# Loading 128 rows at a time and releasing each load by a product's place in its block of 256 TensorE instructions

## The chip, the cores and the metric

The kernel runs on one core of a Trainium2 chip. The metric is the device time of one execution in microseconds (us). TensorE is called PE below (its weight loads PEld), VectorE DVE, ScalarE ACT, GpSimd POOL and SyncE SP. SP computes nothing here: it issues nearly all of the transfers, one behind the other, in the order in which the program lists them.

## The reference, cut to what matters

Block-sparse attention over 4 batches, 8 heads and 768 rows of head size 64, followed by a soft mixture of 8 experts with 4 slots each. Everything is float32.

```python
# attention: blocks of 32 rows; each block sees its neighbours, the first and last block,
# and 3 sampled blocks; the first and the last block of queries see all keys
scores = (1 / sqrt(64)) * q @ k.T
scores = where(mask, scores, -1e9)
attn = softmax(scores)            # per row
x = (attn @ v)                    # -> 3072 x 512
# soft mixture of experts
logits = x @ phi                  # 3072 x 32
d = softmax(logits, axis=0)       # over the 3072 rows
slot_input = d.T @ x              # 32 x 512, 4 slots per expert
h = maximum(slot_input[e] @ w1[e], 0)      # w1: 8 x 512 x 1024
slot_out[e] = h @ w2[e]                    # w2: 8 x 1024 x 512
out = softmax(logits, axis=1) @ slot_out   # 3072 x 512
```

The two weight tensors are 16.8 MB each and are read once. Keys, queries and values are a few MB per batch.

## The kernel before, in words

**Attention.** The four batches run one after the other. A batch has two dense parts (the first and the last block of queries against all keys: products sd at line 730, avd at line 628) and eleven pairs of query blocks. For a pair, POOL and ACT copy the keys that the pair sees into a staging tile (kst, lines 455 to 465) and POOL copies the sampled values (vrs, line 481), PE makes the scores (s, line 536), DVE the maxima, ACT the exponentials, DVE the 32x32 transposes (ptt), and PE the products with the values (av, line 628). Every finished tile of 128 rows of x is transposed on PE (mxt, line 821); groups of four tiles go through the logits and the running softmax over rows (ml, lt, md, ms, lines 856 to 906).

**Loads.** Batch b+1's keys and values are loaded while batch b computes (`plan_loads`, line 415: `load_k` at line 339, `load_v` at line 350). Eleven weight tiles of 512 KB (`NPRE`, pool wpre) are loaded during attention (line 1049). In the last batch, 12 more tiles go into buffers that keys, values and dense probabilities no longer need: 3 in a key buffer (kw), 6 in the first value buffer (v), 3 in ptd (line 1059). After that come 3 tiles in the second key buffer (kw again, in halves of 512 columns) and all the rest, in whatever space the end of attention frees (`load_late`, line 1197, in the order `LORD`). There are 64 weight tiles in all. When attention is over, the experts' products (pf at line 1243, pso at line 1251) follow the arrival of the weights, and the output (po, line 1347) is stored in 26 transfers.

**Order of the work.** `Plan.run` (line 96) lays out the tasks of attention before anything is emitted. Each task has a cost, the engines that may do it, the tasks that it needs, buffers that it takes, and a key. The planner walks through time: at each step it takes, of the tasks that could start first, the one with the lowest key. The key is the task's place (the number n of its pair) plus an offset for its kind from the table `OFF`. So `OFF` decides the order on every engine. The result is an order per engine, written out by hand: SP too issues its transfers in that order.

**Pacing.** Loads with `pace=True` (keys and values of batches 1 to 3, the 11 early weight tiles and the 12 tiles of the last batch) are spread out in two ways. In the plan, the next may start no sooner than bytes / `RATE` after the one before (line 144; `RATE` counts MB per us). In the program, each waits for a PE instruction (lines 196 to 200): the last one of the latest PE task that ends by the plan 1.5 us before the load's planned start. The loads are cut into pieces of `LR` = 32 rows of the 128 (line 419 for keys and values of batch 1 and the keys of the others, line 1049 and 1059 for the weights). The values of batches 2 and 3 are cut in quarters of 32 rows by their layout (line 350), whatever `LR` is. As SP issues in order, what stands behind a waiting load waits too: the query tiles (q, line 330, 128 KB each, four buffers) stand between the paced loads.

Of the kernel before, what the change touches and what calls it, by code (L numbers as in the profile page):

```python
# [40 lines left out]

LD0, LD1 = 3, 12

LR, RATE = 32, 0.22

LC = 512

# [12 lines left out]
H1, HALF = 3, 4  # L60
CPES = [0, 0, 3, 3, 3, 2, 0, 0]
HEAD = -4096
SWITCH = 0.095
BACK = {"PE": 0.17, "DVE": -0.07, "ACT": -0.1, "POOL": -0.06, "SP": 0.0, "NONE": 0.0}
OFF = {"acc": 4.15, "av": 2.35, "av1": 4.1, "av2": -5, "avo": -4.9, "avo1": -5, "ce": 5, "cm": -2.05,
       "cn": 0.65, "dav": 3.7, "davo": -3.85, "dexp": 1.8, "do": 2.9, "dqk": 0.05, "dt": 4.55, "dtop": 0.85,
       "dtrn": -4.55, "exp": 2.7, "fix": 4.3, "ldq": 3.55, "lexp": -1.45, "lg": -0.55, "lo": -2.85, "lp": -5,
       "lt": 5, "ltop": -5, "qk": 0.85, "scl": 3.05, "smp": 3.9, "sum": -3.1, "top": -4.8, "trn": 0.2,
       "vst": 4.7, "xt": -2.8, "xto": -1}
E_ = mybir.EngineType  # L70
MAN = {E_.PE, E_.DVE, E_.Activation, E_.Pool}
LAG = {"PE": 0.28, "DVE": 0.08, "ACT": 0.06, "POOL": 0.1, "SP": 0.0, "NONE": 0.0}
# [10 lines left out]
class Plan:  # L83
# [6 lines left out]
    def add(self, f, opts, deps, key, acq=(), byte=0, pre=None, pace=False, kind=None, mode=None, ni=0):  # L90
        t = Task(f, opts if isinstance(opts, list) else [opts], deps, key + OFF.get(kind, 0.0), acq, byte, pre, pace,
                 kind, mode, ni)
        self.tasks.append(t)
        return t

    def run(self):
        tasks = self.tasks
        at = {e: 0.8 for e in LAG}
        dma = paced = 0.0
        mode = None  # L100
        left = {t: len(t.deps) for t in tasks}
        ready = {t: 0.0 for t in tasks}
        out = {t: [] for t in tasks}
        for t in tasks:
            for d in t.deps:
                out[d].append(t)
        slot = {p: [0.0] * n for p, n in self.pools.items()}
        held = {p: [set() for _ in range(n)] for p, n in self.pools.items()}
        nxt = {p: 0 for p in self.pools}
        queue = {p: sorted([t for t in tasks if any(q == p for q, _ in t.acq)], key=lambda t: t.key)  # L110
                 for p in self.pools if p not in self.free}
        gives = {t: [] for t in tasks}
        spans, open_ = [], {}
        avail = [t for t in tasks if not t.deps]
        order = []
        while avail:
            cand = []
            for t in avail:
                r, ok, k = ready[t], True, {}
                for p, _ in t.acq:  # L120
                    i = (nxt[p] + k.get(p, 0)) % self.pools[p]
                    k[p] = k.get(p, 0) + 1
                    if (p in queue and queue[p][0] is not t) or held[p][i]:
                        ok = False
                        break
                    r = max(r, slot[p][i])
                if ok:
                    if t.pace:
                        r = max(r, paced)

                    st, e, d = min(((max(r, at[e]), e, d) for e, d in t.opts), key=lambda z: (z[0], z[0] + z[2]))
                    if e == "PE" and t.mode and t.mode[0] != mode:
                        d += SWITCH
                    cand.append((st, t.key, st + d, t, e, d))
            assert cand, [(t.key, t.opts) for t in avail][:8]
            soon = min(c[:3] for c in cand)
            eng = min(cand, key=lambda c: c[:3])[4]
            st, _, en, t, e, d = min((c for c in cand if c[4] == eng and c[0] <= soon[0] + 0.05), key=lambda c: c[1:3])
            avail.remove(t)
            if e == "PE":  # L140
                mode = t.mode[-1] if t.mode else None
            t.start, t.eng, at[e] = st, e, en + BACK[e] + (0.11 if t.kind in ("qk", "dqk") else 0.0)
            if t.pace:
                paced = st + t.byte / RATE / 1e6
            if e == "NONE":
                t.fin = st
            elif e == "SP":
                dma = max(dma, st + 2.2) + t.byte / 0.39e6
                t.fin = dma + 1.8
            elif t.kind == "fix":  # L150
                t.fin = st + 0.1
            else:
                t.fin = en
            order.append(t)
            for p in {p for p, _ in t.acq}:
                if p in queue:
                    queue[p].pop(0)
            for p, users in t.acq:
                i = nxt[p]
                nxt[p] = (i + 1) % self.pools[p]  # L160
                held[p][i] = set(users)
                for u in users:
                    gives[u].append((p, i))
                spans.append([p, i, st, 1e9])
                open_[p, i] = spans[-1]
            for p, i in gives[t]:
                held[p][i].discard(t)
                slot[p][i] = max(slot[p][i], t.fin + LAG[e])
                if not held[p][i]:
                    open_[p, i][3] = slot[p][i]  # L170
            for o in out[t]:
                left[o] -= 1
                ready[o] = max(ready[o], t.fin + LAG[e])
                if not left[o]:
                    avail.append(o)
        assert len(order) == len(tasks), len(tasks) - len(order)

        todo = {e: [t for t in order if t.eng == e and t.pre] for e in at}
        pe_end = 0.0
        pe = []  # L180
        for t in order:
            q = todo[t.eng]
            while q and q[0].start <= t.start + 1.6:
                u = q.pop(0)
                u.vals = u.pre(u.eng)
            if t.eng == "PE":

                if (t.start > self.fill[0].fin and t.start - pe_end > 0.45
                        and sum(p == "s" and a < t.start and z > pe_end for p, _, a, z in spans) < SB):
                    self.fill[1](int((t.start - pe_end - 0.15) / 0.28))  # L190
                pe_end = t.fin
            i = t.f(t)
            if t.eng == "PE":
                last = next(i for i in reversed(self.tc.nc.cur_bb.bb.instructions) if i.engine == E_.PE)
                pe.append((t.fin, last.name))
            elif t.pace:

                name = [n for f, n in pe if f <= t.start - 1.5][-1]
                self.tc.add_manual_dep(i.ins, name, mybir.DependencyInfo(
                    mybir.DependencyClass.Sync, mybir.DependencyReason.DATA), reason="pace")  # L200


@with_exitstack
# [1241 lines left out]
```

## Time and profile before

| | |
|---|---|
| time, median of 3 executions | 310.28 us (310.16 to 313.34) |
| the profiled execution, its own time | 308.52 us |
| its span, first to last instruction | 306.7 us |
| mean granted TensorE clock | 0.971 |
| busy: PE, DVE, POOL, ACT | 279.4, 213.5, 179.2, 166.2 us |
| read from HBM, written | 56.19 MB, 6.29 MB |

The time of an execution holds some 1.8 us more than the span of its instructions. Times in the views are counted from the first instruction. A view of windows gives, for each stretch, the busy time of each engine with the number of its instructions in brackets, the granted clock, the mean busy share of the 16 DMA engines and what they moved. In a timeline, instructions of one kind that follow each other are merged to one row: start, length, engine, line, operation, tiles, count, and in square brackets the idle time ahead of them and what ended it ("issue": nothing that the profile shows). Of the transfers' queues, q1 carries the tensors and q8 what is marked "instruction".

### The profile page before, as it was taken

To read this page: it belongs to the slowest core of one execution; us is meant where nothing else is said; L and a number is where in the kernel's file an instruction comes from. 1 tells how busy PE (TensorE), PEld (TensorE's weight loads), DVE (VectorE), ACT (ScalarE), POOL (GpSimd) and SP (SyncE) were. 2 spreads that over 40 slices of the span, in tenths; PEclk is the share of its full clock that TensorE was granted. 3 is DMA by queue.
4 is the path that set the end of the run, shared out by engine and by line. 5 is a ranking of instruction groups with operands and counts; after the bars stand their busy time and mean duration, and the time that the engine had idled before them with its cause. 6 is when DMAs were issued, how large, how long until landed. Compare 5 with 4: busy or idle time off the path is not lost.

```text
span 306.7 us, 17586 instructions
## 1 busy us (share of the span) xinstructions
PE 279.4 (91%) x7159; PEld 194.0 (63%) x7159; DVE 213.5 (70%) x496; ACT 166.2 (54%) x515; POOL 179.2 (58%) x501
## 2 busy tenths in 40 slices
PE   7689997999999999999999999999999899999670
PEld 6249774775786767757777667877767643454260
DVE  4698877567997778998988979988876361113160
ACT  0875856552767787355787754695831421014250
POOL 2669589747947889583599967569657112000000
PEclk9799997999999999999999999999999999999975
DMA  7935667640357661034476320778888999999998
GB/s 245 401 124 165 193 190 215 145 138 5 95 167 210 163 186 38 5 90 141 141 197 175 116 74 21 203 200 228 216 241 286 322 372 366 390 408 408 393 338 286
DMA packets 34227, 63.62 MB, mean 207 GB/s; under 512 B 5602, under 2 KB 19043, under 8 KB 34147
## 3 DMA queue, kind: packets, MB, share of 16 engines
q1 hardware_dynamic: 34000, 62.37, 63.8%
q8 instruction: 56, 0.92, 1.3%
q14 instruction: 25, 0.20, 0.2%
q10 hardware_dynamic: 146, 0.13, 0.1%
HBM read 56.19 MB, written 6.29 MB: 204 GB/s over the span
## 4 chain that ended last, share of the span: by engine, by line
PE 45%; DMA 24%; issue 7%; POOL 6%; POOLq 5%; ACT 4%; DVE 3%; SPq 2%; ACTq 1%
PE av L628 19%; DMA w<-in_w_dram 11%; PE avd L628 7%; DMA v<-in_w_dram 7%; PE s L536 6%; POOLq L362 4%; DMA q<-in_qT_dram 4%; PE sd L730 3%; PE mxt L821 3%; POOL vrs L481 2%; DMA v<-in_vfull_dram 2%; PE po L1347 2%; POOL kst L457 2%; PE ms L906 2%; PE ml L856 2%
## 5 line engine op out<-in xcount | busy, mean ns | idle before, releaser
L481 POOL COPY vrs<-v 128x260 f32 x264 | 95.0, 405 | 27.9 <-PE av L628 19.4
L556 ACT ACTIVATE p<-s,nm 128x256 f32<-128x256 f32 x176 | 72.4, 483 | 12.6 <-DVE nm L551 11.2
L628 PE MATMUL av<-v,ptt 64*64 64x130 f32 (+2 forms) x1728 | 75.6, 287 | 0.3 <-issue 0.3
L628 PEld LDWEIGHTS av<-v,ptt 64*64 64x64 f32 (+2 forms) x1728 | 50.4, 133 | 24.3 <-issue 17.5
L563 DVE STREAM_TRANSPOSE ptt<-p 128x512 f32<-128x512 f32 x88 | 57.6, 689 | 6.2 <-ACT p L556 5.4
L551 DVE TENSOR_REDUCE nm<-s 128x2 f32<-128x512 f32 x88 | 54.9, 679 | 3.1 <-PE s L536 2.5
L536 PE MATMUL s<-kst,q 64*32 64x256 f32 x1408 | 51.2, 385 | 4.8 <-POOL kst L465 2.8
L457 POOL COPY kst<-ktile 128x384 f32<-128x384 f32 x88 | 43.1, 507 | 17.9 <-PE s L536 16.9
L628 PE MATMUL av<-vrs,ptt 64*32 64x130 f32 x2112 | 46.4, 275 | 1.7 <-issue 1.1
L463 ACT ACTIVATE kst<-ktile 128x128 f32 x177 | 40.9, 309 | 11.2 <-PE s L536 9.9
L536 PEld LDWEIGHTS s<-kst,q 64*32 64x32 f32 x1408 | 30.2, 107 | 16.9 <-POOL kst L465 3.4
L628 PEld LDWEIGHTS av<-vrs,ptt 64*32 64x32 f32 x2112 | 35.6, 105 | 4.1 <-issue 2.7
L374 ACT COPY xT<-mxt 128x512 f32<-128x512 f32 (+1 forms) x25 | 14.1, 564 | 30.3 <-PE mxt L821 30.2
L628 PE MATMUL avd<-v,ptd 64*64 64x130 f32 x768 | 23.2, 271 | 2.0 <-DVE x L623 1.8
L628 PEld LDWEIGHTS avd<-v,ptd 64*64 64x64 f32 x768 | 21.8, 132 | 4.0 <-issue 1.6
L465 POOL COPY kst<-ktile 128x128 f32 x87 | 21.9, 294 | 0.5 <-ACT dT L890 0.5
L498 ACT ACTIVATE q<-q 128x256 f32<-128x256 f32 x25 | 10.4, 424 | 17.5 <-DMA q<-in_qT_dram 17.5
L730 PE MATMUL sd<-ktile,q 64*32 64x384 f32 x256 | 18.4, 510 | 0.9 <-ACT p L556 0.5
L761 ACT ACTIVATE pd<-sd,nb 128x384 f32<-128x384 f32 x32 | 16.6, 578 | 2.6 <-DVE nb L756 2.3
L748 DVE TENSOR_REDUCE nm<-sd 128x1 f32<-128x384 f32 x32 | 16.2, 544 | 2.6 <-PE sd L730 2.6
L821 PEld LDWEIGHTS mxt<-ident,x 128*128 128x128 f32 x96 | 10.4, 143 | 11.6 <-issue 3.7
L821 PE MATMUL mxt<-ident,x 128*128 128x128 f32 x96 | 16.3, 292 | 1.1 <-DVE x L610 1.0
(120 smaller groups left out, 276.0 us busy)
## 6 DMA issues: line engine op xcount, KB each, us to landing
q<-in_qT_dram SPq DMA_DIRECT2D x47, 128.0 KB, 2.4
w<-in_w_dram SPq DMA_DIRECT2D x44, 128.0 KB, 3.2
w<-in_w_dram SPq DMA_DIRECT2D x11, 512.0 KB, 10.1
out_dram<-ob SPq DMA_DIRECT2D x22, 256.0 KB, 3.9
ktile<-in_kT_dram SPq DMA_DIRECT2D x48, 96.0 KB, 3.1
w<-in_w_dram SPq DMA_DIRECT2D x18, 256.0 KB, 6.1
v<-in_w_dram SPq DMA_DIRECT2D x24, 128.0 KB, 3.8
v<-in_w_dram SPq DMA_DIRECT2D x12, 256.0 KB, 5.4
```

What stands on the lines that cost most here:

```text
L457: POOL.tensor_copy(out=st[:, :, w:w + 96], in_=kv[:, :, (i - 1) * BLK:(i + 2) * BLK])
L463: ACT.activation(out=st[:, :, o:o + BLK], in_=src, func=AF.Copy, scale=1.0)
L465: POOL.tensor_copy(out=st[:, :, o:o + BLK], in_=src)
L481: POOL.tensor_copy(out=st[:, :, j:j + 1, :], in_=vf[:, :, ds(t.vals[j], 1), :])
L536: PE.matmul(u.s[r][32 * p:32 * p + 32, j, :], lhsT=u.q[s_, p, j, :], rhs=kd[j][0][s_, p, :], start=True, stop=True)
L551: DVE.tensor_reduce(out=u.nm[r], in_=u.s[r], axis=AX.X, op=ALU.max, negate=True)
L556: ACT.activation(out=u.p[r][:, j, :], in_=u.s[r][:, j, :], func=AF.Exp, bias=u.nm[r][:, j:j + 1], scale=1.0)
L563: DVE.transpose(out=T.pt[r][:, :, 2 * w:2 * w + 2, :].rearrange("p k j q -> p j k q"), in_=u.p[r].rearrange("p j (k q) -> p j k q", k=8))
L628: PE.matmul(av[:, r * 2 * D1:(r + 1) * 2 * D1].rearrange("p (a d) -> p a d", a=2), lhsT=lhsT, rhs=rhs, start=start, stop=stop)
L730: PE.matmul(u.s[r][k][32 * p:32 * p + 32, :], lhsT=T.dq.q[s_, p, j, :], rhs=kt[s_, p, 384 * k:384 * (k + 1)], start=True, stop=True)
L761: ACT.activation(out=u.p[r][k], in_=u.s[r][k], func=AF.Exp, bias=u.nb[r], scale=1.0)
L821: PE.transpose(T.px[:, c, :], T.x[:, c * P:(c + 1) * P], ident)
```

## The change

Five things are edited; the tables below are the whole of it.

1. `LR` goes from 32 to 128: a paced load moves all 128 rows at once, 512 KB for a weight tile where it was four pieces of 128 KB, 384 KB for a quarter of a batch's keys where it was four pieces of 96 KB, and so for the values of batch 1. The quarters of the values of batches 2 and 3 stay as they are. `RATE` goes from 0.22 to 0.18.
2. The planner counts PE instructions and keeps, in blocks of 256, a time `fetched`: a PE task that crosses the border of a block is lengthened if `fetched` lies later than the crossing, and each crossing sets `fetched` anew (`FETCH`, 3.5 us after the crossing, at least 3.8 us after the one before).
3. While the program is emitted, each PE instruction is entered in a list with its running number (2 for a transpose, 4 for another product, times `MORE` = 1.0092 for instructions that are not counted) and its planned time.
4. A paced load no longer waits for the end of a task 1.5 us ahead of its planned start. It waits for a product that stands `QUIET` = 50 instructions behind a border (number 191 + 256 k): the latest border that by the plan lies at least 0.3 us ahead of the load's planned start. Loads with planned starts in the same block wait for the same product.
5. All 35 offsets of `OFF` are new, so the order on all the engines is a new one.

```diff
-LR, RATE = 32, 0.22
+LR, RATE = 128, 0.18
+
+FIRST, BLOCK, MORE, QUIET = 191, 256, 1.0092, 50
...
-SWITCH = 0.095
+SWITCH, FETCH = 0.095, (3.5, 3.8)
...
-OFF = {"acc": 4.15, "av": 2.35, "av1": 4.1, "av2": -5, "avo": -4.9, "avo1": -5, "ce": 5, "cm": -2.05,
-       "cn": 0.65, "dav": 3.7, "davo": -3.85, "dexp": 1.8, "do": 2.9, "dqk": 0.05, "dt": 4.55, "dtop": 0.85,
-       "dtrn": -4.55, "exp": 2.7, "fix": 4.3, "ldq": 3.55, "lexp": -1.45, "lg": -0.55, "lo": -2.85, "lp": -5,
-       "lt": 5, "ltop": -5, "qk": 0.85, "scl": 3.05, "smp": 3.9, "sum": -3.1, "top": -4.8, "trn": 0.2,
-       "vst": 4.7, "xt": -2.8, "xto": -1}
+OFF = {"acc": 5, "av": -0.35, "av1": 0.75, "av2": -2.35, "avo": -4.7, "avo1": -3.4, "ce": -1.4, "cm": -1.65,
+       "cn": 5, "dav": 0.8, "davo": 4.5, "dexp": -5, "do": 1.75, "dqk": 0.4, "dt": -1.85, "dtop": -1.55,
+       "dtrn": -2.75, "exp": -5, "fix": -2.75, "ldq": 1.2, "lexp": -1.95, "lg": 5, "lo": 1.85, "lp": 0.05,
+       "lt": -5, "ltop": -4, "qk": -0.05, "scl": 4.55, "smp": -3.85, "sum": 4.45, "top": -2, "trn": -0.15,
+       "vst": -3.7, "xt": 4.6, "xto": 0.05}
...
-        mode = None
+        mode, fetched, count = None, -9.0, 62
...
             if e == "PE":
                 mode = t.mode[-1] if t.mode else None
+                for m in range(count // 256 + 1, (count + t.ni) // 256 + 1):
+                    at_ = st + (en - st) * (256 * m - count) / t.ni
+                    en += max(0.0, fetched - at_)
+                    fetched = max(at_ + FETCH[0], fetched + FETCH[1])
+                count += t.ni
...
-        pe = []
+        pe, seen, count = [], len(self.tc.nc.cur_bb.bb.instructions), 0
...
             if t.eng == "PE":
-                last = next(i for i in reversed(self.tc.nc.cur_bb.bb.instructions) if i.engine == E_.PE)
-                pe.append((t.fin, last.name))
+                made = [i for i in self.tc.nc.cur_bb.bb.instructions[seen:] if i.engine == E_.PE]
+                for m, p in enumerate(made):
+                    count += 2 if p.is_transpose else 4
+                    pe.append((count * MORE, t.start + (t.fin - t.start) * (m + 1) / len(made), p.name))
             elif t.pace:
 
-                name = [n for f, n in pe if f <= t.start - 1.5][-1]
+                marks = [c for c, f, _ in pe if f <= t.start - 0.3 and (c - FIRST) % BLOCK < 4 * MORE]
+                name = next((n for c, _, n in pe if c >= marks[-1] + QUIET), pe[-1][2])
                 self.tc.add_manual_dep(i.ins, name, mybir.DependencyInfo(
                     mybir.DependencyClass.Sync, mybir.DependencyReason.DATA), reason="pace")
+            seen = len(self.tc.nc.cur_bb.bb.instructions)
```

## The prediction, made before the changed kernel was run

> **What bounds the kernel now.** I read the page first, then busy time by stretches, then the chain of waits, and last the idle time ahead of PE's weight loads.
>
> ```profile
> PE 279.4 (91%) x7159; PEld 194.0 (63%) x7159; DVE 213.5 (70%) x496; ACT 166.2 (54%) x515; POOL 179.2 (58%) x501
> ...
> q8 instruction: 56, 0.92, 1.3%
> ```
> ```profile
> 20.00:60.00 40.00, 36.96 (x1096) 27.26 (x1096) 31.03 (x63) 27.41 (x87) 32.47 (x94) 0.96 0.62 175
> 60.00:100.00 40.00, 38.46 (x1148) 28.29 (x1148) 32.93 (x74) 24.74 (x77) 28.05 (x79) 1.00 0.43 122
> 100.00:140.00 40.00, 38.73 (x1178) 27.93 (x1178) 33.68 (x79) 26.46 (x89) 33.19 (x95) 1.00 0.35 99
> 140.00:180.00 40.00, 39.60 (x1237) 29.69 (x1229) 34.49 (x70) 28.04 (x94) 31.55 (x90) 1.00 0.52 149
> 180.00:220.00 40.00, 39.47 (x1229) 29.55 (x1234) 35.50 (x78) 27.13 (x83) 29.28 (x85) 1.00 0.59 160
> 220.00:240.00 20.00, 18.64 (x551) 13.55 (x533) 14.56 (x46) 6.05 (x20) 10.42 (x27) 1.00 0.85 255
> 240.00:260.00 20.00, 19.22 (x178) 10.14 (x180) 7.75 (x32) 6.74 (x20) 4.56 (x8) 1.00 1.03 365
> 270.00:280.00 10.00, 9.73 (x153) 5.52 (x146) 2.00 (x6) 1.84 (x5) 0.00 (x0) 1.00 1.03 408
> ```
>
> There are two stages. From 20 to 240 us PE is busy almost throughout: it is idle for 3.04 us in 20 to 60, and for 1.54 + 1.27 + 0.40 + 0.53 = 3.74 us in the 160 us after. From 240 on the transfers bound: their engines are full (share 1.03) at 365 to 408 GB/s, because most of the weights are still to come. The chain of waits agrees: one transfer of weights after another, from the end of attention to the last products.
>
> ```profile
> 231.83 0.89 PE st L396 x8
> 232.71 7.88 DMA w<-in_w_dram
> ...
> 279.10 10.12 DMA w<-in_w_dram
> 289.27 0.64 PE pso L1251 x8
> ```
>
> The late weights get their space from attention, so the end moves one for one with the end of attention, as long as the same bytes are on board by then.
>
> PE's instructions explain part of its idle time. 7159 weight loads and 7159 products are 14,318 instructions, and q8 carried 56 packets: 255.7 instructions to each, 0.92 MB / 56 = 16 KB. So q8 looks like PE's program arriving in blocks of 256. In the timeline of PE's weight loads, these rows stand in the middle of runs of equal work, where nothing but the program could be missing:
>
> ```profile
> 45.17 0.13 PEld L628 LDWEIGHTS av<-vrs,ptt 64*32 64x32 f32 x2 [0.56 <-issue]
> ...
> 96.85 0.14 PEld L628 LDWEIGHTS av<-vrs,ptt 64*32 64x32 f32 x3 [0.92 <-issue]
> ...
> 112.91 0.24 PEld L628 LDWEIGHTS av<-vrs,ptt 64*32 64x32 f32 x17 [0.49 <-issue]
> ...
> 121.33 0.17 PEld L628 LDWEIGHTS av<-vrs,ptt 64*32 64x32 f32 x12 [0.40 <-issue]
> ...
> 135.69 0.11 PEld L856 LDWEIGHTS ml<-xT,phis 128*32 128x32 f32 x1 [1.04 <-issue]
> ...
> 237.10 0.19 PEld L628 LDWEIGHTS av<-v,ptt 64*64 64x64 f32 x3 [0.59 <-issue]
> ```
>
> Cutting the span at these six places gives the instructions between them:
>
> ```profile
> 45.10:96.80 51.70, 48.55 (x1388) 34.70 (x1389) 39.87 (x85) 33.07 (x101) 37.89 (x109) 0.97 0.48 136
> 96.80:112.85 16.05, 15.85 (x508) 12.19 (x507) 12.28 (x25) 11.97 (x43) 14.28 (x41) 1.00 0.65 178
> 112.85:121.30 8.45, 8.29 (x254) 5.34 (x254) 7.42 (x15) 5.43 (x21) 7.77 (x23) 1.00 0.32 96
> 121.30:135.60 14.30, 13.59 (x374) 9.92 (x375) 12.73 (x36) 6.97 (x17) 9.85 (x28) 1.00 0.17 46
> 135.60:237.05 101.45, 99.99 (x3039) 74.26 (x3038) 87.30 (x193) 64.68 (x209) 75.22 (x211) 1.00 0.59 168
> ```
>
> 2777, 1015, 508, 749 and 6077 are 97.5 to 99.2% of 11, 4, 2, 3 and 24 times 256; the rest would be instructions that this view doesn't count (waits). All six stalls lie on borders of blocks. A border takes 101.45 / 24 = 4.23 us to come round in the last stretch, and its block must have arrived by then. Ahead of two of the stalls SP had just sent a train of pieces:
>
> ```profile
> 91.82 2.41 SPq L344 DMA_DIRECT2D ktile<-in_kT_dram  x5
> ...
> 131.66 2.94 SPq L231 DMA_DIRECT2D w<-in_w_dram  x4
> ```
>
> **Releases at borders (edits 3 and 4): a gain.** The six waits add to 0.56 + 0.92 + 0.49 + 0.40 + 1.04 + 0.59 = 4.00 us. The one at 237 stays: from 226.9 on the loads are not paced. The three large ones (96.85, 112.91, 135.69: 2.45 us) lie where PE is all but full and I count them whole. Those at 45.17 and 121.33 I count half (0.48 us): around the first the chain runs through POOL's copies, and the other block would have been short of time with little beside it. **Taken: 2.9 us gained.** Bounds: none of it, if other borders stall instead; 4.0 us, if all go.
>
> [...]
>
> Does the new release leave room? Fifty instructions are 50/256 x 4.23 = 0.8 us behind the border. The planner's count is somewhat short: 11,126 counted instructions made 44 x 256 = 11,264, a factor of 1.012 against `MORE` = 1.0092, or some 40 instructions (0.6 us) by the end, on the late side, where the fetch is already under way. Beside almost nothing a 128 KB transfer lands in 2.0 us:
>
> ```profile
> DMA packets 468, 0.77 MB, mean 85 GB/s; under 512 B 96, under 2 KB 352, under 8 KB 465
> ...
> q<-in_qT_dram SPq DMA_DIRECT2D x2, 128.0 KB, 2.0
> ```
>
> At 0.377 MB/us (250 to 260 us, row below) a 512 KB piece lasts 1.39 us where 128 KB lasts 0.35, so it lands some 3.1 us after its issue, 3.9 us after the border: before the next at 4.23. Two pieces on one border end near 5.3 and reach 1 us into the next fetch. The spacing by `RATE` is 0.524 / 0.18 = 2.91 us, so 4.23 / 2.91 = 1.45 pieces fall to a block: nearly half the blocks have two. These fetches are later, but meet one end of a load and not a train all the way; I add no cost.
>
> **Pieces of 128 rows (edit 1).** From 190 to 231 us the transfers, nearly all in pieces of 32 rows, fill 75.3% of 41 us for 8.45 MB, 274 GB/s of full use; in 250 to 260, in pieces of 128 rows, it is 377 / 1.04 = 362.
>
> ```profile
> q1 hardware_dynamic: 3820, 8.45, 75.3%
> ```
> ```profile
> 250.00:260.00 10.00, 10.00 (x92) 3.65 (x88) 3.77 (x15) 1.69 (x4) 3.57 (x6) 1.00 1.04 377
> ```
>
> So the same bytes use a quarter less of the transfer engines. SP issues 43 transfers where it issued 172 (keys 48, values of batch 1 32, weights 4 x 23), but SP bounds nothing. Both cost nothing on the path; the first makes the fetches' case better and is already in the 2.9.
>
> **The slower rate (edit 1).** In the last batch 13 tiles (kw 3, w 1, v 6, ptd 3) go out from 191.58 to 226.8:
>
> ```profile
> 191.58 0.89 SPq L231 DMA_DIRECT2D kw<-in_w_dram  x2
> ...
> 219.27 7.53 SPq L231 DMA_DIRECT2D ptd<-in_w_dram  x12
> 226.91 3.81 SPq L231 DMA_DIRECT2D kw<-in_w_dram  x6
> 230.76 9.51 SPq L231 DMA_DIRECT2D w<-in_w_dram  x12
> 240.65 5.16 SPq L231 DMA_DIRECT2D v<-in_w_dram  x8
> ```
>
> That is 35.2 us; the old pace alone asks for 13 x 2.38 = 31.0, the new for 13 x 2.91 = 37.9. A release at the border goes out on average 4.23 / 2 - 0.8 = 1.3 us ahead of its plan, so 36.6 us: some 1.4 us later, 0.26 MB, or 0.7 us at 0.377 MB/us if it is pushed into the full stage. But in 236 to 240 the transfers run below that:
>
> ```profile
> 236.00:238.00 2.00, 1.65 (x56) 1.14 (x59) 0.00 (x0) 0.00 (x0) 1.11 (x3) 1.00 0.73 251
> 238.00:240.00 2.00, 0.99 (x46) 0.75 (x33) 1.15 (x8) 0.00 (x0) 0.00 (x0) 1.00 0.89 268
> ```
>
> 2 x (0.126 + 0.109) = 0.47 MB of room there covers it. **Taken: nothing**; 0.7 us if that room is gone; the nominal 37.9 - 35.2 = 2.7 us would be 1.3 us.
>
> **The new order (edits 2 and 5).** No row tells what another table of offsets does. PE's idle time bounds it on the gain's side: 3.04 + 3.74 less the 3.41 us of the five stalls before 220, some 3.4 us. On the other side I take as much again. **Taken: nothing.**
>
> **The sum**: -2.9 + 0 + 0 = -2.9 us. Against the profiled execution, 308.52 - 2.9 = 305.6; that execution lies 1.76 us below the median of 310.28, to which the same 2.9 us apply: **307.4 us**.
>
> **The rivals.**
>
> (a) The order finds more: the stalls (2.9) and the 3.4 us of other idle time go, 310.28 - 6.3 = **304.0**. For it: PE's idle time in 20 to 60. Against: the last 80 us have only 0.93 left.
>
> (b) Slower: large pieces in front of the queries. A q behind two pieces of 512 KB waits 2 x 1.39 = 2.8 us for them instead of 0.35, so lands 2.4 later. q is awaited already:
>
> ```profile
> ACT q L498 <- DMA q<-in_qT_dram: 17.5, 9, 3.5
> ...
> POOL q L500 <- DMA q<-in_qT_dram: 12.2, 8, 3.6
> ```
>
> Of these 17, 45% (8) would stand behind a pair; if a third of the delay reaches PE, 8 x 2.4 / 3 = 6.4 us: 307.4 + 6.4 = **313.8**. It decides once a q lands later than the key copies of its pair, on ACT and POOL behind it. Against: no wait of PE is put down to it today.
>
> (c) The fetch was covered, or its stalls only move to other borders or to POOL: **310.3**.
>
> (d) The releases slip: if the uncounted instructions are many more in the new order, pieces go out 1.4 us behind the border or later and still collide, and the late loads (1.3 us) join: **311.6**.
>
> **How the numbers follow.** The measurement tells 1% from no change, so faster means below 307.2 and slower above 313.4. Forecast 0.50, with its own range 305 to 309.5: 0.23 faster, 0.27 same. (a) 0.18, faster. (b) 0.17, slower. (c) 0.10: 0.08 same, 0.02 slower. (d) 0.05: 0.02 same, 0.03 slower. Together 0.41 faster, 0.37 same, 0.22 slower. The range goes from a little below (a), 302.5, to a little above (b), 314.5.
>
> **What would show it.** Right: the waits for "issue" of 0.4 us and more in the middle of runs are gone up to 226 us; PE's idle time in 60 to 220 falls from 3.74 to about 2; attention, and the chain's first transfer of weights (232.7), end 3 us earlier; from there on the rows look the same. Wrong: such waits at other borders; more idle time of ACT and POOL for q and of PE behind them; the second kw later than 229; or a start of the weight chain that moved without the stalls having gone, which would be the order's doing.

## The result and the profile after

The changed kernel takes 312.87 us (median of 20 executions, 309.55 to 315.38) against 310.08 for the kernel before (20 executions, 308.30 to 314.76): 1.007 times as long, 95% interval 1.0044 to 1.0096. It is slower, by less than 1%, where 307.4 us was forecast. The profiled execution took 312.06 us with a span of 310.3. The ratios here and below compare only executions within 1.5% of each kernel's fastest, so they need not equal the quotient of the medians, and where one execution is very fast they rest on few.

The page of the changed kernel, and its busy time by stretches (busy times, instructions, granted clock, transfer share, GB/s):

```profile
PE 277.6 (89%) x7159; PEld 193.3 (62%) x7159; DVE 218.4 (70%) x503; ACT 165.4 (53%) x517; POOL 177.3 (57%) x492
...
q1 hardware_dynamic: 31936, 62.36, 60.1%
```
```profile
20.00:60.00 40.00, 37.80 (x1244) 29.43 (x1233) 34.39 (x68) 28.00 (x91) 34.52 (x99) 0.99 0.64 197
60.00:100.00 40.00, 37.90 (x1152) 27.33 (x1146) 33.48 (x75) 24.44 (x78) 27.83 (x78) 1.00 0.39 117
100.00:140.00 40.00, 38.43 (x1198) 27.60 (x1194) 35.51 (x80) 27.82 (x92) 30.21 (x85) 1.00 0.36 101
140.00:180.00 40.00, 37.87 (x1128) 26.68 (x1118) 31.96 (x68) 26.49 (x89) 30.30 (x85) 0.96 0.43 126
180.00:220.00 40.00, 37.15 (x1111) 27.59 (x1117) 33.02 (x72) 23.30 (x71) 25.26 (x70) 0.96 0.44 145
220.00:240.00 20.00, 19.37 (x578) 14.27 (x559) 17.25 (x46) 8.78 (x28) 15.01 (x41) 1.00 0.71 229
240.00:260.00 20.00, 17.51 (x225) 10.32 (x227) 8.45 (x37) 5.65 (x18) 4.44 (x8) 1.00 1.02 365
```

From 60 to 220 us PE is idle for 2.10 + 1.57 + 2.13 + 2.85 = 8.65 us, where it was 3.74: 4.9 us more. Before it, 20 to 60 got better (2.20 idle after 3.04), and behind it 220 to 240 (0.63 after 1.36), in which the later attention is still at work. The last stage is as full of transfers as before (share 1.02 after 1.03 from 240 to 260 us, 365 GB/s in both); it starts later (its first train of more than eight late pieces leaves at 236.55 us, where it left at 230.76).

The idle time ahead of PE's weight loads, the rows of 0.6 us and more in the middle of runs of equal work:

```profile
34.16 0.18 PEld L639 LDWEIGHTS av<-vrs,ptt 64*32 64x32 f32 x15 [1.09 <-issue]
42.57 0.16 PEld L639 LDWEIGHTS av<-vrs,ptt 64*32 64x32 f32 x9 [0.62 <-issue]
54.67 1.45 PEld L547 LDWEIGHTS s<-kst,q 64*32 64x32 f32 x57 [1.04 <-issue]
63.24 0.18 PEld L639 LDWEIGHTS av<-vrs,ptt 64*32 64x32 f32 x14 [0.69 <-issue]
...
85.75 1.01 PEld L547 LDWEIGHTS s<-kst,q 64*32 64x32 f32 x38 [1.50 <-issue]
...
133.45 0.58 PEld L547 LDWEIGHTS s<-kst,q 64*32 64x32 f32 x22 [1.63 <-issue]
...
167.57 0.16 PEld L639 LDWEIGHTS av<-vrs,ptt 64*32 64x32 f32 x5 [2.36 <-issue]
...
200.68 1.26 PEld L547 LDWEIGHTS s<-kst,q 64*32 64x32 f32 x49 [2.95 <-issue]
...
210.51 1.03 PEld L547 LDWEIGHTS s<-kst,q 64*32 64x32 f32 x42 [0.64 <-issue]
```

These nine add to 12.52 us, where the six of before (0.40 us and more) had 4.00. They too lie on borders of blocks. Cut at them, the stretches between hold 508, 761, 509, 1268, 2789, 2030, 1775 and 507 counted instructions, 99.0 to 99.4% of 2, 3, 2, 5, 11, 8, 7 and 2 times 256. The first and the fifth of them:

```profile
34.10:42.50 8.40, 8.06 (x254) 6.20 (x254) 6.69 (x12) 4.44 (x15) 6.15 (x17) 1.00 0.76 231
85.70:133.40 47.70, 45.92 (x1395) 31.98 (x1394) 41.51 (x88) 32.56 (x107) 37.88 (x106) 1.00 0.40 112
```

The stalls on the borders, which the change was to end, have grown. The longest can be followed. SP's timeline of the changed kernel ahead of it:

```profile
191.23 1.59 SPq L242 DMA_DIRECT2D kw<-in_w_dram  x1
192.92 0.37 SPq L341 DMA_DIRECT2D q<-in_qT_dram  x1
193.34 2.38 SPq L242 DMA_DIRECT2D kw<-in_w_dram  x2
201.80 0.33 SPq L341 DMA_DIRECT2D q<-in_qT_dram  x1
```

Three pieces of 512 KB and a query tile leave within 4.5 us. The border before the stall lies near 194.2: from there to 197.74, where PE stops, 259 instructions are counted. So the third piece (at 195.40) leaves behind this border, but the second, which stands behind a query tile in SP's order, leaves only 0.9 us ahead of it. The transfers' queues from 194.2 to 198.2 us, and then from 198.2 to 200.7:

```profile
q1 hardware_dynamic: 460, 1.30, 96.3%
```
```profile
q1 hardware_dynamic: 79, 0.25, 26.2%
q8 instruction: 1, 0.02, 2.4%
```

In the first 4 us q1 fills the engines (96.3%) and q8 moves nothing. Its next packet begins at 198.3, as the last of the three pieces runs out, and PE goes on at 200.68, 2.4 us later. In this case the block of instructions didn't pass the data that was on the way. At the second longest stall q8's packet begins at 164.9, behind data at 84.1% of the engines from 162.0 to 164.5, and PE goes on 2.7 us later, at 167.57. The two packets, in windows of 0.1 us:

```profile
q8 instruction: 1, 0.02, 60.1%
```
```profile
q8 instruction: 1, 0.02, 79.6%
```

Both of these stalls cost more than their idle time: behind each, the granted clock is at half for some 3 us while PE is busy.

```profile
167.50:171.00 3.50, 3.42 (x69) 2.81 (x69) 2.14 (x5) 0.29 (x1) 3.43 (x11) 0.52 0.03 6
201.60:205.00 3.40, 3.40 (x48) 2.13 (x36) 2.98 (x5) 2.96 (x13) 2.89 (x8) 0.53 0.43 93
```

That is 3.50 x 0.48 + 3.40 x 0.47 = 3.3 us, an estimate. It isn't what parts the kernels: the kernel before has such a stretch too (0.50 from 50 to 53 us), the mean clock of the 20 executions is 0.975, and in a later job the 29 of the kernel before have 0.975 as well.

### The profile page after: what moved, and what is told of

Read it like the earlier page. It is cut to its first block, busy times and chain, and to the rows that moved or that the text cites. A ratio compares the mean times of both kernels' runs of the same rounds, so it can differ in the third digit from the quotient of the medians.

```text
span 310.3 us, 17377 instructions
## 1 busy us (share of the span) xinstructions
PE 277.6 (89%) x7159; PEld 193.3 (62%) x7159; DVE 218.4 (70%) x503; ACT 165.4 (53%) x517; POOL 177.3 (57%) x492
## 3 DMA queue, kind: packets, MB, share of 16 engines
q1 hardware_dynamic: 31936, 62.36, 60.1%
## 4 chain that ended last, share of the span: by engine, by line
PE 70%; DMA 11%; issue 5%; DVE 4%; ACT 3%; POOL 2%; POOLq 1%; ACTq 1%; SPq 0%; DVEq 0%
PE av L639 31%; PE s L547 14%; PE avd L639 7%; DMA w<-in_w_dram 7%; PE mxt L832 4%; DMA v<-in_w_dram 3%; PE sd L741 3%; PE st L407 3%; PE ml L867 2%; PE pf L1254 2%; PE ms L917 2%; DMA out_dram<-ob 1%; PE po L1358 1%; ACT p L567 1%; ACT kst L474 1%
## 5 line engine op out<-in xcount | busy, mean ns | idle before, releaser
L567 ACT ACTIVATE p<-s,nm 128x256 f32<-128x256 f32 x176 | 70.9, 476 | 25.4 <-DVE nm L562 22.2
L639 PE MATMUL av<-v,ptt 64*64 64x130 f32 (+2 forms) x1728 | 76.7, 290 | 0.7 <-PE sd L741 0.6
L547 PE MATMUL s<-kst,q 64*32 64x256 f32 x1408 | 53.9, 393 | 8.4 <-issue 5.4
L474 ACT ACTIVATE kst<-ktile 128x128 f32 x186 | 42.8, 304 | 17.2 <-PE s L547 12.8
L547 PEld LDWEIGHTS s<-kst,q 64*32 64x32 f32 x1408 | 32.2, 108 | 21.6 <-issue 9.4
L476 POOL COPY kst<-ktile 128x128 f32 x78 | 19.8, 294 | 1.2 <-ACT kst L474 0.7
L385 ACT COPY xT<-mxt 128x512 f32<-128x512 f32 (+1 forms) x18 | 10.0, 558 | 18.1 <-PE mxt L832 18.0
L511 POOL TENSOR_SCALAR q<-q 128x256 f32<-128x256 f32 x23 | 9.2, 406 | 14.7 <-DMA q<-in_qT_dram 13.3
L634 DVE TENSOR_TENSOR x<-av,rs 128x512 f32<-128x512 f32 (+1 forms) x27 | 16.5, 612 | 1.1
L776 DVE STREAM_TRANSPOSE ptd<-pd 128x384 f32<-128x384 f32 x32 | 16.2, 551 | 1.1 <-ACT pd L772 0.9
```

The costliest lines, as they stand in the source:

```text
L474: ACT.activation(out=st[:, :, o:o + BLK], in_=src, func=AF.Copy, scale=1.0)
L476: POOL.tensor_copy(out=st[:, :, o:o + BLK], in_=src)
L547: PE.matmul(u.s[r][32 * p:32 * p + 32, j, :], lhsT=u.q[s_, p, j, :], rhs=kd[j][0][s_, p, :], start=True, stop=True)
L567: ACT.activation(out=u.p[r][:, j, :], in_=u.s[r][:, j, :], func=AF.Exp, bias=u.nm[r][:, j:j + 1], scale=1.0)
L634: DVE.tensor_tensor(out=x, in0=a[:, :, :, 0:D], in1=rs[lo:hi].unsqueeze(3).to_broadcast([hi - lo, 2, 2 * n, D]), op=ALU.mult)
L639: PE.matmul(av[:, r * 2 * D1:(r + 1) * 2 * D1].rearrange("p (a d) -> p a d", a=2), lhsT=lhsT, rhs=rhs, start=start, stop=stop)
```

## The experiments

Three columns of the table are read from views. "PE waits" is the sum of the waits of PE's products that ended by "issue", from 20 to 245 us, in the profiled execution. "Lands" is the median time from issue to landing of a piece of a weight tile (w), from 20 to 235 us. "Moved" is what q1 moved from 20 to 235 us, in MB. Medians run over all executions. The profiled executions of e10_cols2, e14_hybrid, e15_after and e16_small took 315.92, 310.91, 313.65 and 309.17 us, longer than their kernels' medians. The expectations count waits another way than the table, with higher figures: 4.8 us for the kernel before (table: 2.3) and 16 for the changed kernel (10.4). So their bounds on waits can be held against the column only roughly.

| kernel | order | piece, release, rate | median, of before in the same job (us) | ratio (95%) | PE waits | lands | moved |
|---|---|---|---|---|---|---|---|
| before | old | 32 rows, old, 0.22 | 310.08 | 1 | 2.3 | 3.2 | 30.90 |
| e13_before | old | the same, again | 310.71 (one execution) | | 6.0 | 3.2 | 30.22 |
| e1_order | new | 32 rows, old, 0.22 | 308.99, 311.75 | 0.996 (0.992 to 1.000) | 4.0 | 3.4 | 30.85 |
| e17_small22 | new | 32 rows, border, 0.22 | 309.28, 310.68 | 0.997 (0.993 to 1.002) | 5.5 | 3.2 | 31.57 |
| e4_small | new | 32 rows, border, 0.18 | 308.20, 311.75 | 0.989 (0.985 to 0.993) | 3.6 | 3.0 | 30.36 |
| e16_small | new | the same, again | 308.54, 310.68 | 0.993 (0.989 to 0.998) | 6.2 | 3.3 | 30.40 |
| e11_spread | new | 32 rows, spread, 0.18 | 309.29, 310.43 | 1.004 (0.999 to 1.009) | 4.3 | 3.2 | 30.55 |
| e8_rel | old | 32 rows, border, 0.22 | 311.87, 310.66 | 0.999 (0.994 to 1.004) | 6.6 | 3.0 | 29.75 |
| e12_old18 | old | 32 rows, border, 0.18 | 309.04, 310.43 | 1.003 (0.997 to 1.008) | 6.1 | 3.2 | 30.97 |
| e5_cols | new | a quarter of the columns, border, 0.18 | 310.50, 310.66 | 0.996 (0.992 to 1.001) | 4.6 | 3.5 | 30.16 |
| e10_cols2 | new | half of the columns, border, 0.18 | 311.09, 310.43 | | 9.4 | 3.7 | 29.58 |
| e14_hybrid | new | 128 rows at 0.12, last batch 32 rows at 0.18 | 309.26, 310.68 | 0.997 (0.992 to 1.001) | 6.1 | 4.1 | 29.95 |
| e7_slow | new | 128 rows, border, 0.12 | 310.57, 310.66 | 0.999 (0.995 to 1.003) | 6.0 | 4.1 | 29.68 |
| after | new | 128 rows, border, 0.18 | 312.87, 310.08 | 1.007 (1.004 to 1.010) | 10.4 | 4.5 | 29.70 |
| e15_after | new | the same, again | 312.06, 310.68 | | 12.9 | 4.6 | 29.66 |
| e2_pacing | old | 128 rows, border, 0.18 | 312.19, 311.75 | 1.002 (0.998 to 1.006) | 11.2 | 4.6 | 30.10 |
| e9_lr64 | new | 64 rows, border, 0.18 | 315.19, 310.66 | 1.016 (1.010 to 1.021) | 12.7 | 4.8 | 29.12 |
| e3_oldrel | new | 128 rows, old, 0.18 | 323.54, 311.75 | 1.042 (1.035 to 1.048) | 15.7 | 5.0 | 28.21 |

The waits of PE in five of these profiles (in us, times, longest): before, before again, 32 rows with the new order and release (e16_small), after, and 128 rows with the old release (e3_oldrel):

```profile
PE av L628 <- issue: 1.5, 4, 0.6
PE ml L856 <- issue: 0.8, 1, 0.8
```
```profile
PE av L628 <- issue: 4.6, 9, 0.9
PE ml L856 <- issue: 1.0, 1, 1.0
PE avd L628 <- issue: 0.4, 1, 0.4
```
```profile
PE mxt L832 <- issue: 3.1, 1, 3.1
PE av L639 <- issue: 2.1, 5, 0.8
PE s L547 <- issue: 1.0, 3, 0.5
```
```profile
PE s L547 <- issue: 5.4, 5, 2.5
PE av L639 <- issue: 4.3, 5, 2.1
PE mxt L832 <- issue: 0.7, 2, 0.6
```
```profile
PE s L547 <- issue: 8.6, 7, 2.7
PE av L639 <- issue: 6.6, 8, 2.4
PE mxt L832 <- issue: 0.5, 1, 0.5
```

Single waits of 2 to 3 us on the ordinary products (s, av) stand only in kernels with large pieces (2.1 to 2.7 in after, e2_pacing and e3_oldrel; with 32 rows 1.8 at the most); the one of 3.1 us with 32 rows lies at 229.6 us, among loads that are not paced.

The time goes with the waits only in part, and at least as closely with the last column. The prediction had set the condition for it: "as long as the same bytes are on board by then". The seven profiles that had moved 30.36 MB or more by 235 us have spans of 303.9 to 307.7 us; the six with 29.70 MB or less have 310.3 to 322.3. In e7_slow the waits are short (6.0 us), but 29.68 MB had moved, and its span is 310.3 us like that of the changed kernel. A kernel that is late has also moved less by a fixed moment, so the column is a sign and not shown to be a cause.

**Order and pacing apart.** The new order alone:

```diff
-LR, RATE = 128, 0.18
+LR, RATE = 32, 0.22
...
+                name = [n for _, f, n in last if f <= t.start - 1.5][-1]
```

Expected: 

> The new order alone: pieces of 32 rows, rate 0.22 and the old release (last PE task that ends 1.5 us ahead of the planned start); the order on PE and DVE is that of the changed kernel. Theory (large pieces and shared releases put more bytes on the way at once, PE's next block of instructions waits behind them, and the new order hid a part of that loss): the mid-run waits for issue, 13 us in the changed kernel before 220 us, fall to 3 to 5 us, and the time is 303 to 307 us, below before. Rival A (the new order is worse, the pacing is innocent): 312 us or more. Rival B (both are about neutral): 309 to 311 us.

Measured: 308.99 us against 311.75, ratio 0.996 (0.992 to 1.000). Better than the changed kernel, but outside the theory's range and at the edge of rival B's; the order is not to blame.

And the new pacing with the old order (`OFF` of before, without the line that lengthens PE tasks for the fetch):

Expected: 

> The new pacing alone: pieces of 128 rows, rate 0.18, releases 50 instructions behind a border, with the offsets of before and without the fetch in the plan; the order on PE and DVE is that of before. Theory: mid-run waits of 10 us and more as in the changed kernel, 315 to 320 us, slower than the changed kernel. Rival A (the order is to blame): 306 to 309 us. Rival B: 309 to 311 us.

Measured: 312.19 against 311.75, 1.002. The waits came back as foreseen (11.2 us), but the time did not follow: in the old order the whole pacing costs nothing that shows (0.998 to 1.006). The number of the theory was wrong here.

**Size and release.** The changed kernel with the old release, and then with pieces of 32 rows:

```diff
-                name = next((n for c, _, n in pe if c >= marks[-1] + QUIET), pe[-1][2])
+                name = [n for _, f, n in last if f <= t.start - 1.5][-1]
```

Expected: 

> The changed kernel with the old release (last PE task that ends 1.5 us ahead of the planned start), still 128 rows, rate 0.18 and the same order on all engines. Theory in the form that the size of the pieces does it: 311 to 314 us, with mid-run waits of 9 us and more. Rival (the release at the border does it, because it sends loads off together and in front of a border): 305 to 308 us, with waits below 5 us.

Measured: 323.54 us, 1.042, far above both expectations, with the most waits of all (15.7 us). For large pieces the release at the border is worth 3.4% (1.042 to 1.007). The rival, that the release sends loads into the border, has fallen.

```diff
-LR, RATE = 128, 0.18
+LR, RATE = 32, 0.18
```

Expected: 

> The changed kernel with pieces of 32 rows again, at rate 0.18 and with the new release at the border; order on PE and DVE as in the changed kernel. If the bytes that share a release do it, whatever their cutting: 310 to 313 us and mid-run waits of 9 us and more. If the size of a single transfer does it: 304 to 308 us and waits below 5 us.

Measured: 308.20 against 311.75, 0.989 (0.985 to 0.993), waits 3.6 us. One number undone makes the change a gain, as the second reading expected (its upper end was 308). Again, beside the changed kernel on one chip:

Expected: 

> The changed kernel itself, on the same chip as the run with 32 rows below: 1.003 to 1.012 of before, border waits of 13 to 18 us if they belong to the program.

Expected: 

> The changed kernel with pieces of 32 rows (rate 0.18, release at the border) once more. If the size of the pieces is what makes the change slower: 0.988 to 0.998 of before and at least 0.7% below the changed kernel beside it, border waits of 7 to 11 us. If the first run's 0.989 was chance: within 0.4% of the changed kernel.

Measured: 312.06 and 308.54 us, 3.5 us apart, with 12.9 and 6.2 us of waits; the small pieces stand at 0.993 (0.989 to 0.998) of before. PE's sums from 60 to 220 us say the same, the small pieces first:

```profile
sum 160.00, PE 157.16 PEld 114.76 DVE 139.42 ACT 105.02 POOL 119.42; mean PE 39.29 PEld 28.69 DVE 34.85 ACT 26.25 POOL 29.85
```
```profile
sum 160.00, PE 150.08 PEld 107.90 DVE 134.26 ACT 102.70 POOL 114.35; mean PE 37.52 PEld 26.98 DVE 33.56 ACT 25.68 POOL 28.59
```

PE is idle for 2.84 us there with small pieces and for 9.92 with large ones. So, in the new order, the size of the pieces makes the loss. The version with small pieces is the best here: it beats both kernels.

The release on the kernel before, everything else as it was:

Expected: 

> The kernel before with nothing but the new release: same pieces of 32 rows, same rate 0.22, the same order on every engine, and each paced load waits for the product 50 instructions behind the border. Theory (the release itself is a small gain while the pieces are small): 0.985 to 0.997 of before, border waits down from 4.8 to 2 to 4 us. Rival (four pieces that share a release are as bad as one of 512 KB): 1.003 to 1.02, waits of 9 us and more.

Measured: 311.87 against 310.66, 0.999 (0.994 to 1.004): with small pieces the release makes no difference that shows, which is neither the theory's range nor the rival's. The same comes out of the pair e1_order and e17_small22, which differ in the release alone:

Expected: 

> The new order and the release at the border with pieces of 32 rows at the old rate of 0.22: 0.988 to 0.998 if neither rate nor release matters much while the pieces are small; above 1.002 if the rate of 0.18 was what helped; its pair with the old release is the order alone (0.996).

Measured: 309.28 against 310.68, 0.997 (0.993 to 1.002).

**What about the size?** First 64 rows (`LR` = 64):

Expected: 

> The changed kernel with pieces of 64 rows (256 KB for a weight tile), rate 0.18, release at the border, the same order on PE and DVE. Theory (size of one transfer): between the runs with 32 and 128 rows, 0.993 to 1.003 of before, border waits of 10 to 14 us. Rival (only a piece that outlasts its block hurts): like 32 rows, 0.985 to 0.993 and below 10 us.

Measured: 315.19, 1.016 (1.010 to 1.021), worse than 128 rows. Both ranges of the time are missed, though the waits (12.7 us) are the theory's: bytes per transfer alone isn't it. Then the same bytes in another shape, cut by columns so that each piece covers all 128 rows:

```diff
-        for r in range(0, P, LR):
-            add(lambda t, m=m, r=r: load_w(m, wpre, None, slice(r, r + LR)), ("SP", 0.45),
+        for r in range(0, WP, WP // CC):
+            add(lambda t, m=m, r=r: load_w(m, wpre, None, slice(0, P), slice(r, r + WP // CC)), ("SP", 0.45),
```

(`CC` = 4 or 2; keys, values of batch 1 and the late tiles in the same way.)

Expected: 

> As the previous run with pieces of 32 rows (rate 0.18, release at the border, the same order on PE, DVE, ACT and POOL), but the paced loads are cut into four pieces by columns, each of all 128 rows: 128 KB that lie as 8 rows of 1 KB on each of the 16 transfer engines, where 32 rows lie as 2 of 4 KB. Theory (what one transfer puts on the way at once, in bytes, delays the fetch): like that run, 0.985 to 0.995 of before, sum of border waits 6 to 10 us. Rival (the number of rows per transfer engine, or using all 128 rows as such, makes the loss): 1.003 to 1.012 as the changed kernel, waits of 13 us and more.

Expected: 

> Pieces of 256 KB as in the run with 64 rows, but cut by columns, so that each covers all 128 rows (8 rows of 2 KB per transfer engine); rate 0.18, release at the border, the same order on PE and DVE. Theory (pile-up: SP puts out a transfer every 0.45 us; what the engines can't carry in that time piles up ahead of PE's fetch; 128 KB pass, 256 and 512 KB pile up): between four column pieces (0.996) and 512 KB (1.007), 0.997 to 1.006, border waits 11 to 15 us. Rival (it was the use of 64 rows, a half of the partitions, that made the run with 64 rows so slow, 1.016): no worse than 0.996, with waits below 11 us.

Measured: 128 KB by columns 310.50 against 310.66, 0.996; 256 KB by columns 311.09 against 310.43, without a ratio. The waits are 4.6 and 9.4 us. The first is just above the theory's range and clear of the rival's; of the second, the quotient of the medians (1.002) lies in the theory's range, and the waits do not. The rows per transfer engine in both texts are rows divided by 16, an estimate; what shows is the number of packets on q1 from 20 to 235 us: 32,955 and 20,419, with 16,631 for pieces of 32 rows (e4_small). Landing times of one piece of a weight tile, in the runs with 32, 64 and 128 rows (after) and with a quarter and a half of the columns:

```profile
w<-in_w_dram SPq DMA_DIRECT2D x44, 128.0 KB, 3.0
```
```profile
w<-in_w_dram SPq DMA_DIRECT2D x22, 256.0 KB, 4.8
```
```profile
w<-in_w_dram SPq DMA_DIRECT2D x11, 512.0 KB, 4.5
```
```profile
w<-in_w_dram SPq DMA_DIRECT2D x44, 128.0 KB, 3.5
```
```profile
w<-in_w_dram SPq DMA_DIRECT2D x22, 256.0 KB, 3.7
```

256 KB on 64 rows take 4.8 us to land, on 128 rows 3.7. What makes the difference is not shown. The waits of PE follow the landing time better than the size: 3.0 to 3.5 us go with 2.3 to 6.6 us of waits, 4.1 with 6.0 and 6.1, 4.5 to 5.0 with 10.4 to 15.7; 256 KB by columns (3.7 and 9.4) is the one that doesn't fit.

**One or two to a border.** The rate at 0.12 puts about one piece of 512 KB on a block (0.524 / 0.12 = 4.4 us from one to the next, where a border comes round in 4.23; an estimate):

Expected: 

> The changed kernel with the rate at 0.12, so that by the plan the next piece of 512 KB follows 4.4 us after the one before, about one to a block of 4.2 us. If pairs and triples of pieces on one border delay the fetch, and a single piece of 512 KB has room: the border waits fall from 16 to below 9 us. If a single piece is too much already: they stay at 12 us or more. The time cannot be read for that alone, since the last batch's 13 tiles need 19 us longer by the plan: between 308 and 320 us.

Measured: the waits fall from 10.4 to 6.0 us, the time to 310.57 against 310.66, although the last batch's loads go out much later. So a piece alone brings no more waits than small ones do. That pairs make them is the likely reading; the slower rate also leaves fewer pieces on the way at any time. With the 12 last tiles in pieces of 32 rows, so that they are not late:

```diff
-                paced = st + t.byte / RATE / 1e6
+                paced = st + t.byte / (RATE if t.byte == 131072 else SLOW) / 1e6
...
-            parts = [(slice(r, r + LR), slice(0, WP)) for r in range(0, P, LR)]
+            parts = [(slice(r, r + 32), slice(0, WP)) for r in range(0, P, 32)]
```

Expected: 

> The changed kernel with rate 0.12 for the pieces of 128 rows, one to a block, and the 12 tiles of the last batch in pieces of 32 rows at rate 0.18; release at the border, order on PE as in the changed kernel. Theory (a single 512 KB piece behind a border has room; pairs don't, and late loads cost at the end): border waits of 7 to 11 us, the last batch's loads in time, 0.983 to 0.995 of before. Rival (a piece of 512 KB is too much in any case): 1.000 to 1.010, waits of 13 us and more.

Measured: 309.26 against 310.68, 0.997 (0.992 to 1.001), waits 6.1 us: between the two ranges of the time, with short waits as the theory has it, and no better than 32 rows throughout.

**The rest.** A release of its own for each small piece, kept away from the borders:

Expected: 

> Pieces of 32 rows, rate 0.18, the new order, but a release of its own for each piece: the product that by the plan ends 0.3 us ahead of the piece's planned start, moved only if it lies less than 50 instructions behind a border or less than 90 ahead of the next. Theory (pile-up): pieces spread over the middle of a block leave less on the way at a border, border waits 4 to 8 us, 0.980 to 0.990 of before. Rival (four pieces at 0.45 us from each other on one release are spread enough): the same as with the shared release, 0.986 to 0.993 and 8 to 10 us.

Measured: 309.29 against 310.43, ratio 1.004 (0.999 to 1.009); waits 4.3 us. By the medians (0.996) it is no better either: no gain over the shared release, and neither range met. The old order with rate 0.18 and the border:

Expected: 

> The offsets of before, no fetch in the plan, with pieces of 32 rows, rate 0.18 and release at the border: what the order adds to the best run so far (0.989). If the new order is worth something: 0.996 to 1.002 here. If all comes from rate and release: 0.986 to 0.992.

Measured: 309.04 against 310.43, ratio 1.003 (0.997 to 1.008). Inconclusive: against the same pacing with the new order (0.989 and 0.993) the new order is worth 1% or more by the ratios, but by the medians (0.996 against 0.989 and 0.993) 0.3 to 0.7%. Beside e2_pacing (1.002), which differs in the size alone, the old order shows no loss from large pieces in the ratios and 0.5% in the medians (0.996 and 1.001). And the kernel before once more:

Expected: 

> The kernel before once more, for the spread of its own border waits: its profile had 4.8 us of them in an execution of 308.5 us, faster than most. If the waits differ from one execution to the next, this one has 6 to 9 us in an execution of 309.5 to 312 us; if they belong to the program, 4 to 5.5 us whatever its time.

Measured: 6.0 us of PE waits in an execution of 310.71 us, after 2.3 in one of 308.52. The waits of one and the same program differ that much.

## Why the prediction was wrong, point by point

**What bounds the kernel** was read rightly. The changed kernel's long stalls lie on borders of 256 instructions as well, and the end follows the end of attention: in the chain of the changed kernel PE leads up to 261 us, and from there on it is one transfer of weights after another, as before:

```profile
261.01 9.74 DMA w<-in_w_dram
...
281.03 10.66 DMA w<-in_w_dram
```

The last of them ends at 281.03 + 10.66 = 291.7 us, against 279.10 + 10.12 = 289.2 before: 2.5 us of the 3.6 us by which the span grew.

**The failing step is the room behind the border, and the second piece taken at nothing.** The prediction let a 512 KB piece land 3.1 us after its issue, 3.9 us after the border, before the next one at 4.23, and for the blocks with two pieces it said "I add no cost". A piece landed after 4.5 us (median) in the changed kernel; with the 0.8 us of the release that is 5.3, behind the next border already. The 3.1 (2.0 + 1.39 - 0.35 = 3.04) came from a rate of 0.377 MB/us, taken from a stage where many transfers are in flight; one piece from issue to landing doesn't reach it (0.524 MB in 4.5 us, 0.117 MB/us).

The next border was not the right mark either: in the two stalls above PE went on 2.4 and 2.7 us after q8's packet began, so the packet has to begin within 4.23 - 2.5 = 1.7 us of its border, an estimate. In the profile of before, q8's next packet began 1.3 to 2.0 us after PE went on at the borders at 96.85, 112.91, 121.33 and 135.69 us, and 4.0 and 3.1 us after those at 45.17 and 237.10. So 1.4 us behind a border, where the prediction had the fetch "already under way" (0.8 us and the 0.6 of the short count), the packet had begun in one case of six. A late landing alone doesn't make long waits, though: with about one piece to a block (e7_slow) it is 4.1 + 0.8 = 4.9 us, and the waits are 6.0 us as with small pieces. What failed most is therefore the term for several pieces near one border, taken at nothing: in the case shown above q8 was silent for 4 us with three of them on the way. Rival (d), large pieces that slip and still collide, has a part in this, as the second of the three pieces left 0.9 us ahead of a border; its 311.6 us lies 1.3 from the measured 312.87. How the stalls turn into time is not shown step by step.

**The stalls to be gained were mis-sized as well.** 2.9 us of 4.00 rested on one execution, of 308.52 us. They were not removed: with the release alone (e8_rel) PE waits 6.6 us, against 2.3 and 6.0 in two profiles of before. Term: -2.9 forecast; with small pieces the ratio of 0.999 (0.994 to 1.004) shows nothing; with pieces of 128 rows the waits grew by 4 to 11 us (10.4 and 12.9 after 2.3 and 6.0).

**Pieces of 128 rows** were costed at nothing, with the remark that they use a quarter less of the transfer engines. Less is right, a quarter is too much. Over the span q1's share is 60.1% after and 63.8% before (first line); from 190 to 231 us, where the prediction took 274 GB/s of full use, the changed kernel (second line) has 7.20 MB / (0.529 x 41 us) = 332 GB/s, so 17% less engine time for a byte.

```profile
q1 hardware_dynamic: 34000, 62.37, 63.8%
```
```profile
q1 hardware_dynamic: 2651, 7.20, 52.9%
```

It doesn't help: by the waits, what counts is how full the way is when a border comes (96.3% and 84.1% of the engines ahead of the two longest). Beside each other, 128 and 32 rows differ by 3.5 us.

**The slower rate** was costed at nothing on the path. No run shows a cost of 0.18: with small pieces 0.18 (0.989, 0.993) is no worse than 0.22 (0.997).

**The new order**, taken at nothing, points to a small gain: e1_order's 0.996 (0.992 to 1.000) has it alone, and with the release at the border and rate 0.22 the new order stands at 0.997 (0.993 to 1.002) beside 0.999 for the old, which shows no difference. In sum: order some -1 to -3 us, release and rate nothing that shows, size +3.5 us, together +0.5 to +2.5; the change came out at 312.87 - 310.08 = +2.8 us by the medians and 0.7%, 2.2 us, by the ratio.

**Rival (b)** (queries behind large pieces, 313.8) was the nearest in time, by luck, and wrong in cause. The waits of the changed kernel for q are

```profile
POOL q L511 <- DMA q<-in_qT_dram: 13.3, 8, 3.4
...
ACT q L509 <- DMA q<-in_qT_dram: 6.4, 5, 2.2
```

where they were 12.2 and 17.5 us: in sum less than before. Rival (c) (310.3: the fetch covered, or its stalls only moved) does not hold here: PE's waits of 10 us and more (10.4 to 15.7) go with large pieces of data.

Left open: why half of the growth in waits does not appear in the time (waits 6.7 us apart between e15_after and e16_small, medians 3.5), and why the old order takes large pieces with less loss (1.002) than the new (1.007), although it waits as long. The bytes on board by 235 us go the same way in the second case (30.10 MB in e2_pacing, 29.70 in the changed kernel), but no run changes them alone.

## What to carry to other kernels

Here a long unrolled program competed with its own data (q8 silent for 4 us while q1 moved 1.30 MB). So look for waits on "issue" inside runs of equal work, and count the instructions between them. Before a load is made larger to be efficient (332 GB/s of full use here, after 274), check how long one takes to land in this very stage, not at the full rate, and how many can stand near one border: here about one piece of 512 KB to a block brought no more waits than pieces of 128 KB, and more of them did. Count beside the waits what has been loaded by the end of the stage. And profile a kernel twice before a term of 1% is built on a single execution's stalls.

## What was not expected of the hardware

From 194.2 to 198.2 us of the changed kernel no packet of PE's instructions (q8) moved while 1.30 MB of data passed (96.3% of the transfer engines), so in this case they did not go ahead of the data. Behind the two longest waits of PE's products in the changed kernel (2.1 and 2.5 us) the granted clock was 0.52 and 0.53 for some 3.5 us; behind the gaps of 1.50 and 1.63 us ahead of its weight loads at 85.75 and 133.45 us it stayed at 1.00. 256 KB on 64 rows landed 1.1 us later than 256 KB on 128 rows (4.8 in e9_lr64, 3.7 in e10_cols2). And the border waits of one unchanged program were 2.3 us in one execution and 6.0 in another.
